# Windowed and pooled attention with a gated token mixer: query blocks of 122 with halo keys, band mask on GpSimd, transposed token mix, three-stage batch order

## The chip, the cores and the metric

The kernel runs on one core of a Trainium2 chip. The metric is the device time of one execution in microseconds (us). A core has TensorE (PE, matmuls, with a row of its own for weight loads, PEld), VectorE (DVE), ScalarE (ACT), GpSimd (POOL) and SyncE (SP), each with an instruction queue of its own that it works off in order. Matmuls write PSUM, the other engines read it and write SBUF.

## The reference

Eight batches of 576 tokens, 8 heads of 64. Attention has two parts that are added: one on tokens averaged in fours (144 positions, result repeated four times), one in which a token sees only tokens less than 4 away. The result, heads side by side, is `x` of a gated token mixer.

```python
q_d, k_d, v_d = (t.reshape(B, H, 144, 4, D).mean(axis=3) for t in (q, k, v))
out_up = np.repeat(sm_attn(q_d, k_d, v_d), 4, axis=2)      # softmax attention, scale 1/8
mask = np.abs(pos[:, None] - pos[None, :]) < 4
out_local = softmax(where(mask, q @ k.T / 8, -1e9)) @ v
x = (out_up + out_local), heads side by side: (8, 576, 512)
theta = x @ w_theta
y = w_tok_r @ (x * cos(theta)) + w_tok_i @ (x * sin(theta))   # over tokens, 576 x 576
u = x + y
out = u + maximum(u @ w_ch, 0)
```

## The kernel before, in words

All loads go through POOL's queue and turn float32 into bfloat16 on the way. First come the weights, then for each batch `q_tm`, `k_tm` and `v_tm`, 5 DMAs each (line 151), in pieces of 128 tokens on the partitions. `work` tiles have two buffers, so the load of batch b + 2 waits until batch b has used its tile.

`attention(b)` for one batch:

- Lines 165 and 170: for each pair of heads of q and k five transposes into `pstr` and, with the same data as weights, five matmuls against the pooling matrix `pool4` into `psd`. DVE copies both to SBUF (`sbT`, line 178, and `sbTd`, line 179).
- Line 191: pooled v, `psvd`. Lines 215 and 223: scores of the pooled attention `psSd` and their exps `pdT` on ACT, in key groups of 64 and 80 positions. Line 244: `psnd`, for each head two matmuls of 65 columns (64 of v and a column of ones for the sum), one with 64 and one with 80 rows of keys.
- Lines 276 to 295: for each of 5 key chunks of 128 (the last 64) the scores of up to 134 queries, `psS`, transposed: keys on partitions. Line 284 adds the band mask (0 or -1e9) by a matmul of the identity with `maskv`, four a chunk. ACT takes the exps into `pmain`.
- Line 314: `psup` repeats the pooled result fourfold by a matmul. Lines 338 and 340: `psloc`, the local result of a chunk of queries, four heads to a PSUM tile. A query near a chunk's start also needs the last keys of the chunk before: for chunks 1 to 4 every matmul with 128 (or 67) columns of weights is followed by one with 6, which adds into the first 6 rows. A matmul of zeros (`zrow`) closes the group.
- Lines 347 to 355: DVE divides by the sum and adds `psup`, giving `x`.

`moe(b)`: `x` is transposed (`xTps`, 369), theta is `psth` (386), cos and sin on ACT (394, 395), `zr` and `zi` on DVE, the token mix `psu` (412) is 5 output chunks of 10 matmuls of 512 columns, `u` on DVE (419), transposes `uTps` (428), `psr` (443), relu and sum on DVE (450), the write of `osb` on SP's queue (454).

The order is made by generators: each `yield` ends a step, and the loop at the end takes one step of `attention(b)`, one of `moe(b - 1)` and, at the start of a batch, up to 3 of `attention(b + 1)` in turn. The tile framework puts in the waits and may move instructions a little within an engine. PSUM has 8 banks: 6 tiles `w1` and 2 tiles `tr`.

## Time and profile before

| | us |
|---|---|
| median of 3 runs | 581.99 (580.44 to 582.56) |
| span of the profiled execution | 579.8 |
| PE busy | 529.4 (91%) |
| DVE, ACT, POOL busy | 256.9, 138.1, 115.6 |

PE stands for 82% of the chain of work that ended last. The sums for PE count time in which at least one matmul was in the pipeline, at whatever clock was granted; a granted clock of 1.00 is 2.4 GHz, 0.50 is 1.2 GHz.

### The profile page before, as it was taken

What the parts mean: (1) busy time and instruction counts of PE and PEld (TensorE: products, weight loads), DVE (VectorE), ACT (ScalarE), POOL (GpSimd) and SP (SyncE); (2) the same over time, 40 slices, a digit from 0 to 9 for tenths busy, and PEclk for the clock granted to TensorE, in tenths of its full rate; (3) what the DMA queues carried; (4) which work ended last, traced back from release to release, by engine and by line L of the source; (5) the groups of instructions that cost most, each with busy time, mean ns of one, the idle gap of its engine ahead of it and who ended that gap; (6) DMA issues with size and microseconds to landing.
All of it is one profiled execution on the core that took longest, in us unless ns stands there. A gap on an engine that the chain in (4) does not pass through costs nothing.

```text
span 579.8 us, 8334 instructions
## 1 busy us (share of the span) xinstructions
PE 529.4 (91%) x3386; PEld 291.3 (50%) x3386; DVE 256.9 (44%) x776; ACT 138.1 (24%) x384; POOL 115.6 (20%) x156
## 2 busy tenths in 40 slices
...
GB/s 81 173 144 143 22 55 2 81 15 69 42 36 46 75 42 9 82 36 48 41 42 42 72 17 35 1 3 80 42 1 0 37 47 0 1 9 74 2 6 75
DMA packets 120054, 26.50 MB, mean 46 GB/s; under 512 B 113232, under 2 KB 115408, under 8 KB 120016
## 3 DMA queue, kind: packets, MB, share of 16 engines
...
q14 instruction: 12, 0.10, 0.1%
...
## 4 chain that ended last, share of the span: by engine, by line
PE 82%; DVE 7%; DMA 6%; ACT 2%; POOL 1%; issue 1%; DVEq 0%; POOLq 0%
PE psu L412 22%; PE psloc L338 13%; PE psth L386 9%; PE psnd L244 7%; PE pstr L165 4%; PE psr L443 4%; DMA out_dram<-osb 4%; PE psup L314 3%; PE psd L170 3%; PE psS L284 3%; PE xTps L369 3%; PE psS L276 2%; PE psSd L215 2%; DVE sbT L178 2%; PE psvd L191 2%; PE psloc L340 2%
## 5 line engine op out<-in xcount | busy, mean ns | idle before, releaser
L338 PE MATMUL psloc<-v_tm,pmain 128*128 128x65 bf16 (+2 forms) x576 | 87.0, 218 | 4.4 <-DVE osb L450 4.4
L295 ACT ACTIVATE pmain<-psS 128x402 bf16<-128x402 f32 (+5 forms) x160 | 46.4, 375 | 171.8 <-PE psS L284 171.6
L419 DVE TENSOR_TENSOR u<-psu,x 128x512 bf16<-128x512 f32 (+2 forms) x40 | 27.6, 691 | 116.8 <-PE psu L412 116.8
L151 POOL DMA_DIRECT2D v_tm<-in_v_dram x40 | 33.9, 899 | 222.5 <-PE psloc L340 222.5
L338 PEld LDWEIGHTS <-pmain 128*128 128x128 bf16 (+2 forms) x576 | 54.9, 100 | 41.4 <-issue 12.5
L412 PE MATMUL psu<-zr,wrT 128*128 128x512 bf16 (+8 forms) x200 | 70.9, 502 | 0.0
L412 PE MATMUL psu<-zi,wiT 128*128 128x512 bf16 (+8 forms) x200 | 68.7, 489 | 0.0
L394 ACT ACTIVATE cos<-psth,pihc 128x512 bf16<-128x512 f32 (+2 forms) x40 | 28.0, 699 | 154.8 <-PE psth L386 154.8
L386 PE MATMUL psth<-wth,xT 128*128 128x512 bf16 (+2 forms) x160 | 56.8, 508 | 3.3 <-DVE xT L376 3.3
L223 ACT ACTIVATE pdT<-psSd 80x144 bf16<-80x144 f32 (+1 forms) x128 | 27.8, 285 | 84.7 <-PE psSd L215 84.2
L151 POOL DMA_DIRECT2D q_tm<-in_q_dram x40 | 34.2, 936 | 65.5 <-PE psSd L215 65.3
L443 PE MATMUL psr<-wch,uT 128*128 128x512 bf16 (+2 forms) x160 | 45.7, 388 | 1.0 <-DVE uT L435 0.3
L412 PEld LDWEIGHTS <-wiT 128*128 128x128 bf16 (+8 forms) x200 | 28.3, 142 | 36.2 <-issue 25.3
L450 DVE SCALAR_TENSOR_TENSOR osb<-psr,u 128x512 f32<-128x512 f32 (+2 forms) x40 | 27.1, 691 | 35.7 <-DMA out_dram<-osb 19.2
L244 PE MATMUL psnd<-vdext,pdT 64*72 64x65 bf16 (+1 forms) x256 | 42.5, 230 | 0.0
L178 DVE COPY sbT<-pstr 128x576 bf16<-128x576 bf16 x64 | 28.5, 453 | 25.6 <-PE pstr L165 20.6
L412 PEld LDWEIGHTS <-wrT 128*128 128x128 bf16 (+8 forms) x200 | 24.6, 137 | 25.3 <-issue 16.8
L347 DVE RECIPROCAL rl<-psloc 128x4 f32<-128x4 f32 (+2 forms) x80 | 14.3, 179 | 51.7 <-PE psloc L340 50.9
L244 PEld LDWEIGHTS <-pdT 64*72 64x72 bf16 (+1 forms) x256 | 29.1, 113 | 14.9 <-issue 3.7
L151 POOL DMA_DIRECT2D k_tm<-in_k_dram x40 | 34.4, 942 | 8.4 <-PE psd L170 8.4
L386 PEld LDWEIGHTS <-xT 128*128 128x128 bf16 (+2 forms) x160 | 20.8, 145 | 26.6 <-issue 12.1
L349 DVE TENSOR_TENSOR asm<-psloc,rl 128x256 bf16<-128x256 f32 (+2 forms) x80 | 30.5, 411 | 0.7
...
## 6 DMA issues: line engine op xcount, KB each, us to landing
...
```

The source lines that it names most:

```text
L151: nc.gpsimd.dma_start(out=dst[0:rows, c, :, 0:D], in_=src[b, :, 128 * c:128 * c + rows, :].rearrange("h p d -> p h d"),)
L178: nc.vector.tensor_copy(out=sb, in_=ps[:, 0:S])
L223: nc.scalar.activation(out=pd[0:kcnt, SD * (2 * hh + par):SD * (2 * hh + par) + SD], in_=psSds[hh][par][0:kcnt, :], func=AF.Exp, scale=SCL,)
L244: nc.tensor.matmul(out=psn[0:QD, 65 * hj:65 * hj + 65], lhsT=PdT[kk][0:kcnt, colbase:colbase + QD], rhs=vd_ext[kk].rearrange("p (h e) -> p ...
L295: nc.scalar.activation(out=outap[0:kw], in_=psSv[0:kw, :, :], func=AF.Exp, scale=SCL,)
L338: nc.tensor.matmul(out=o, lhsT=lt, rhs=rh, start=(imm == 0), stop=False)
L349: nc.vector.tensor_tensor(out=tmp[0:cnt, :], in0=plv[0:cnt, :, 0:D], in1=rl[0:cnt, 4 * beta:4 * beta + 4].unsqueeze(2).to_broadcast([cnt, ...
L386: nc.tensor.matmul(out=psth[0:cnt, :], lhsT=xT[dc][:, c, 0:cnt], rhs=wth[dc], start=(dc == 0), stop=(dc == 3),)
L394: nc.scalar.activation(out=ct[0:cnt], in_=psth[0:cnt], func=AF.Sin, bias=pihc[0:cnt], scale=1.0)
L412: nc.tensor.matmul(out=psu[0:cnt, :], lhsT=wt[0:TOK_CNT[g], TOK_START[c]:TOK_START[c] + cnt], rhs=zt[0:TOK_CNT[g], :], start=(j == 0), sto ...
L419: nc.vector.tensor_tensor(out=ut[0:cnt], in0=psu[0:cnt], in1=x_tiles[b][c][0:cnt], op=ALU.add)
L443: nc.tensor.matmul(out=psr[0:cnt, :], lhsT=uT[dc][:, c, 0:cnt], rhs=wch[dc], start=(dc == 0), stop=(dc == 3),)
```

## The change

- **Blocks of queries with their own keys.** The 576 queries are cut into blocks of 122 (`QS`, `QC`). Each block has its own window of up to 128 keys, from 3 before its first query to 3 after its last (`KS`, `KW`), so a block needs no keys of another. `psloc` has 8 matmuls a block, all of the same shape, and no closing matmul. v is loaded in these windows (`v_w`).
- **Band mask on POOL.** The mask matmuls are gone. ACT takes the exps of a block's 8 heads in one instruction, and two `affine_select` on POOL then write zeros on either side of the band.
- **Transposes and pooling in one matmul.** q and k are loaded 96 tokens to a piece; the matmul's moving operand `ip` is the identity and the pooling matrix side by side, 120 columns. ACT copies the transposed part, DVE the pooled one.
- **Pooled attention** in two equal key groups of 72; exps of three head pairs at once; pooled v by six masks `PM`.
- **Token mix transposed.** `psu` comes out with model columns on partitions and tokens along the free dimension, 288 at a time: the weights are `z`, the moving operand is the transposed token matrix `WT`. So `u` needs no transpose before `psr`; for the output it is transposed back (`psx`), relu goes to ACT, and DVE adds the two.
- **Order.** The batches run in three stages, `attention(b + 1)`, `modulate(b)` and `mix(b - 1)`, whose steps are taken in the order of the string `PERIOD`. The loads of a batch are issued when the attention of the batch before begins; those of batch 0 stand first in the program, ahead of the constants and the weights.
- **PSUM**: two tiles of two banks (`w2`: `pstr`, `psSd`, `psS`, `psnd`, `psloc`) and four of one (`w1`: all others).

```diff
 DM = 512
 SD = S // 4
 QD = 72
-NEG = -1.0e9
 PIH = math.pi / 2.0
 SCL = 1.0 / 8.0
 
-TOK_START = [0, 125, 253, 381, 509]
-TOK_CNT = [125, 128, 128, 128, 67]
+
+QS = [0, 122, 244, 366, 488]
+QC = [122, 122, 122, 122, 88]
+KS = [0, 119, 241, 363, 485]
+KW = [128, 128, 128, 128, 91]
+QN = [128, 128, 128, 128, 88]
 NCH = 5
-KW = [128, 128, 128, 128, 64]
-NCOL = [TOK_CNT[c] + (6 if c < 4 else 0) for c in range(NCH)]
-CW = 134
-KD_START = [0, 64]
-KD_CNT = [64, 80]
+TR = 96
+NTR = S // TR
+TP = TR // 4
+TW = TR + TP
+
+OS = [0, 128, 256, 384, 512]
+OC = [128, 128, 128, 128, 64]
 
...
-    psw = ctx.enter_context(tc.tile_pool(name="psw", bufs=6, space=bass.MemoryType.PSUM))
-    pst = ctx.enter_context(tc.tile_pool(name="pst", bufs=2, space=bass.MemoryType.PSUM))
+    ps2 = ctx.enter_context(tc.tile_pool(name="ps2", bufs=2, space=bass.MemoryType.PSUM))
+    ps1 = ctx.enter_context(tc.tile_pool(name="ps1", bufs=4, space=bass.MemoryType.PSUM))
+
...
+    def load(b):
+        q_tm = work.tile([TR, NTR, H, D], BF16, tag="q_tm", name=f"q_tm{b}")
+        k_tm = work.tile([TR, NTR, H, D], BF16, tag="k_tm", name=f"k_tm{b}")
+        v_w = work.tile([P, NCH, H, 66], BF16, tag="v_w", name=f"v_w{b}")
+        for dst, src in ((q_tm, q), (k_tm, k)):
+            for c in range(NTR):
+                nc.gpsimd.dma_start(
+                    out=dst[:, c, :, :],
+                    in_=src[b, :, TR * c:TR * c + TR, :].rearrange("h p d -> p h d"),
+                )
+        for c in range(NCH):
+            nc.gpsimd.dma_start(
+                out=v_w[0:KW[c], c, :, 0:D],
+                in_=v[b, :, KS[c]:KS[c] + KW[c], :].rearrange("h p d -> p h d"),
+            )
+        nc.vector.memset(v_w[:, :, :, 64:65], 1.0)
+        return q_tm, k_tm, v_w
+
+    inputs = {0: load(0)}
...
+    ip = const.tile([TR, TW], BF16, name="ip")
+    nc.vector.tensor_copy(out=ip[:, 0:TR], in_=ident[0:TR, 0:TR])
+    nc.gpsimd.memset(ip[:, TR:TW], 0.25)
+    nc.gpsimd.affine_select(out=ip[:, TR:TW], in_=ip[:, TR:TW], compare_op=ALU.is_ge, fill=0.0,
+                            base=0, pattern=[[-4, TP]], channel_multiplier=1)
+    nc.gpsimd.affine_select(out=ip[:, TR:TW], in_=ip[:, TR:TW], compare_op=ALU.is_ge, fill=0.0,
+                            base=3, pattern=[[4, TP]], channel_multiplier=-1)
...
+        if b + 1 < B:
+            inputs[b + 1] = load(b + 1)
...
+        for n, (tm, To, Tdo) in enumerate(((q_tm, qT, qdT), (k_tm, kT, kdT))):
+            for hh in range(4):
+                ps = w2(f"pstr{n}{hh}_{b}")
+                for c in range(NTR):
+                    nc.tensor.matmul(
+                        out=ps[:, c // 3, (c % 3) * TW:(c % 3) * TW + TW],
+                        lhsT=tm[:, c, 2 * hh:2 * hh + 2, :],
+                        rhs=ip,
                         start=True, stop=True,
+                    )
+                pv = ps[:, :, 0:3 * TW].rearrange("p k (c w) -> p k c w", w=TW)
+                nc.scalar.copy(
+                    out=To[:, hh, :].rearrange("p (k c w) -> p k c w", k=2, c=3),
+                    in_=pv[:, :, :, 0:TR],
+                )
+                nc.vector.tensor_copy(
+                    out=Tdo[:, hh, :].rearrange("p (k c w) -> p k c w", k=2, c=3),
+                    in_=pv[:, :, :, TR:TW],
+                )
+                yield
...
+        for kk in range(2):
+            ps = w2(f"psSd{kk}_{b}")
+            for hh in range(3):
+                pooled_scores(lambda par: ps[0:QD, par, SD * hh:SD * hh + SD], kk, hh)
+            nc.scalar.activation(
+                out=pd[:, kk, 0:6, :].rearrange("p (j e) w -> p e j w", e=2),
+                in_=ps[0:QD, :, 0:3 * SD].rearrange("p e (j w) -> p e j w", w=SD),
+                func=AF.Exp, scale=SCL,
+            )
...
+        pms = []
+        for c in range(NCH):
+            kw, qn = KW[c], QN[c]
+            ps = w2(f"psS{c}_{b}")
+            for hh in range(4):
                 for par in range(2):
+                    nc.tensor.matmul(
+                        out=ps[0:kw, par, P * hh:P * hh + qn],
+                        lhsT=kT[64 * par:64 * par + 64, hh, KS[c]:KS[c] + kw],
+                        rhs=qT[64 * par:64 * par + 64, hh, QS[c]:QS[c] + qn],
                         start=True, stop=True,
+                    )
+            pm = work.tile([P, 8, P], BF16, tag="pm", bufs=6, name=f"pm{c}_{b}")
+            nc.scalar.activation(
+                out=pm[0:kw, :, 0:qn],
+                in_=ps[0:kw].rearrange("p e (j w) -> p (e j) w", w=P)[:, :, 0:qn],
+                func=AF.Exp, scale=SCL,
+            )
+            off = KS[c] - QS[c] + 3
+            nc.gpsimd.affine_select(out=pm[0:kw, :, 0:qn], in_=pm[0:kw, :, 0:qn],
+                                    compare_op=ALU.is_ge, fill=0.0,
+                                    base=off, pattern=[[0, 8], [-1, qn]], channel_multiplier=1)
+            nc.gpsimd.affine_select(out=pm[0:kw, :, 0:qn], in_=pm[0:kw, :, 0:qn],
+                                    compare_op=ALU.is_ge, fill=0.0,
+                                    base=6 - off, pattern=[[0, 8], [1, qn]], channel_multiplier=-1)
+            pms.append(pm)
+            yield
...
+                    nc.tensor.matmul(
+                        out=pv[0:QD, h // 4, h % 4, :],
+                        lhsT=pd[:, kk, h, QD * g:QD * g + QD],
+                        rhs=vd[:, kk, h, 0:65],
+                        start=(h % 4 == 0 and kk == 0), stop=(h % 4 == 3 and kk == 1),
+                    )
...
+                nc.tensor.matmul(
+                    out=up[0:qn, :],
+                    lhsT=RT[g][:, QS[c]:QS[c] + qn],
+                    rhs=xd[:, g, :],
+                    start=(g == g0), stop=(g == g1),
+                )
+            ps = w2(f"psloc{c}_{b}")
+            pv = ps[:, :, 0:260].rearrange("p e (j w) -> p e j w", w=65)
+            for par in range(2):
+                for j in range(4):
+                    nc.tensor.matmul(
+                        out=pv[0:qn, par, j, :],
+                        lhsT=pms[c][0:kw, 4 * par + j, 0:qn],
+                        rhs=v_w[0:kw, c, 2 * j + par, 0:65],
+                        start=(j == 0), stop=(j == 3),
...
+            rl = work.tile([P, 2, 4], FP32, tag="rl", name=f"rl{c}_{b}")
+            nc.vector.reciprocal(out=rl[0:cnt], in_=pv[0:cnt, :, :, 64])
+            tmp = work.tile([P, DM], BF16, tag="tmp", name=f"tmp{c}_{b}")
+            nc.vector.tensor_tensor(
+                out=tmp[0:cnt].rearrange("p (j e d) -> p e j d", e=2, j=4),
+                in0=pv[0:cnt, :, :, 0:D],
+                in1=rl[0:cnt].unsqueeze(3).to_broadcast([cnt, 2, 4, D]),
+                op=ALU.mult,
+            )
+            x = xpool.tile([P, DM], BF16, tag="x", bufs=11, name=f"x{c}_{b}")
+            nc.vector.tensor_tensor(out=x[0:cnt], in0=tmp[0:cnt], in1=up[0:cnt], op=ALU.add)
+            xt.append(x)
...
+        uT = moep.tile([P, 4, S], BF16, tag="uT", name=f"uT{b}")
         for dc in range(4):
+            pss = [w1(f"psu{dc}{hf}_{b}") for hf in range(2)]
+            for c in range(NCH):
+                for ri in range(2):
+                    for hf in range(2):
+                        nc.tensor.matmul(
+                            out=pss[hf][:, 0:288],
+                            lhsT=z[0:QC[c], c, ri, P * dc:P * dc + P],
+                            rhs=WT[0:QC[c], ri, c, 288 * hf:288 * hf + 288],
+                            start=(c == 0 and ri == 0), stop=(c == NCH - 1 and ri == 1),
+                        )
+                if c == 2:
+                    yield
+            for hf in range(2):
+                nc.vector.tensor_tensor(
+                    out=uT[:, dc, 288 * hf:288 * hf + 288], in0=pss[hf][:, 0:288],
+                    in1=xT[:, dc, 288 * hf:288 * hf + 288], op=ALU.add,
+                )
+            yield
...
+            nc.scalar.activation(out=rel[0:cnt], in_=psr[0:cnt], func=AF.Relu)
+            osb = moep.tile([P, DM], FP32, tag="osb", bufs=3, name=f"osb{c}_{b}")
+            nc.vector.tensor_tensor(out=osb[0:cnt], in0=rel[0:cnt], in1=psx[0:cnt, 0:DM], op=ALU.add)
+            nc.sync.dma_start(out=out[b, OS[c]:OS[c] + cnt, :], in_=osb[0:cnt])
...
+    PERIOD = (
+        "m a a m x m a a m x m a a m x m a a m x m a m "
+        "a x a a a x a a x a a x a x a x a a x a a x a a x a x a"
+    ).split()
+
+    def run(a, m, x):
+        gens = {"a": a, "m": m, "x": x}
+        for s in PERIOD:
+            g = gens[s]
+            if g is not None:
+                next(g, 0)
+        for s in ("m", "x", "a"):
+            if gens[s] is not None:
+                drain(gens[s])
+
+    a0 = attention(0)
+    wt = build_WT()
+    for _ in range(10):
+        next(a0, 0)
+        next(wt, 0)
+    drain(wt)
+    drain(a0)
+    for b in range(B + 1):
+        run(attention(b + 1) if b + 1 < B else None,
+            modulate(b) if b < B else None,
+            mix(b - 1) if b >= 1 else None)
```

What stands on PE where local attention is computed, before: the end of one `psloc` tile, the `psup` of the next and its first matmuls (`pmain`: exps of a key chunk, two of them by turns; `rt`: the repeating matrix).

```order
L338 MATMUL psloc_3_3178<-v_tm_1856,pmain_3_3016 128x65
L338 LDWEIGHTS pmain_3_2987
L338 MATMUL psloc_3_3178<-v_tm_1856,pmain_3_2987 6x65
L340 LDWEIGHTS zrow
L340 MATMUL psloc_3_3178<-zrow 128x1
L314 LDWEIGHTS rt_107
L314 MATMUL psup_3_3188<-xd_3_2852,rt_107 128x256
L338 LDWEIGHTS pmain_3_3016
L338 MATMUL psloc_3_3190<-v_tm_1856,pmain_3_3016 128x65
L338 LDWEIGHTS pmain_3_2987
L338 MATMUL psloc_3_3190<-v_tm_1856,pmain_3_2987 6x65
```

And in the changed kernel, at the end of one `psloc` tile: `psloc` of attention for batch 2, `psr` of the mix for batch 0.

```order
L310 MATMUL psloc_2_1423<-v_w_571,pm_2_1266 128x65
L395 LDWEIGHTS uT_1022
L395 MATMUL psr_0_1438<-wch,uT_1022 128x512
...
L401 MATMUL psx_0_1443<-ident,uT_1022 128x128
L310 LDWEIGHTS pm_2_1279
L310 MATMUL psloc_2_1456<-v_w_571,pm_2_1279 128x65
...
L300 LDWEIGHTS rt_145
L300 MATMUL psup_2_1453<-xd_1333,rt_145 128x512
L300 LDWEIGHTS rt_149
L300 MATMUL psup_2_1453<-xd_1333,rt_149 128x512
```

The 6-column matmuls and the zero matmul between the others are gone, and whole groups of the mix of an earlier batch stand between the groups of attention.

On POOL, in the middle of the program, before:

```order
L151 DMA v_tm_1856<-in_v_dram 128x8x64 x4
L151 DMA v_tm_1856<-in_v_dram 64x8x64
L151 DMA q_tm_3380<-in_q_dram 128x8x64 x4
L151 DMA q_tm_3380<-in_q_dram 64x8x64
L151 DMA k_tm_3381<-in_k_dram 128x8x64 x4
L151 DMA k_tm_3381<-in_k_dram 64x8x64
```

And in the changed kernel (`pm_3` are the five blocks of batch 3, `v_w_1545` is v of batch 4, `q_tm_2116` and `k_tm_2117` are of batch 5):

```order
L82 DMA v_w_1545<-in_v_dram 128x8x64 x4
L82 DMA v_w_1545<-in_v_dram 91x8x64
L77 DMA q_tm_2116<-in_q_dram 96x8x64 x6
L77 DMA k_tm_2117<-in_k_dram 96x8x64 x6
L260 AFFINE_SELECT pm_3_1816<-pm_3_1816 128x1024
L260 AFFINE_SELECT pm_3_1839<-pm_3_1839 128x1024
L263 AFFINE_SELECT pm_3_1816<-pm_3_1816 128x1024
L263 AFFINE_SELECT pm_3_1839<-pm_3_1839 128x1024
L260 AFFINE_SELECT pm_3_1852<-pm_3_1852 128x1024
```

The selects stand in one queue with the loads of later batches, behind loads that wait for their buffers.

On DVE the tail of attention before, for chunks 2 and 3 of batch 2 (`x_2_243` and `x_3_244` are those chunks, `psloc` comes in halves of four heads):

```order
L347 RECIPROCAL rl_2_2377<-psloc_2_2394 128x4
L347 RECIPROCAL rl_2_2412<-psloc_2_2415 128x4
L349 TENSOR_TENSOR asm_2_2409<-psloc_2_2394,rl_2_2377 128x256
L349 TENSOR_TENSOR asm_2_2438<-psloc_2_2415,rl_2_2412 128x256
L355 TENSOR_TENSOR x_2_243<-asm_2_2409,psup_2_2391 128x256
L355 TENSOR_TENSOR x_3_244<-asm_2_2438,psup_2_2413 128x256
```

And in the changed kernel, for two blocks of batch 3 beside the output of batch 1:

```order
L317 RECIPROCAL rl_3_1988<-psloc_3_1979 122x8
L317 RECIPROCAL rl_3_2005<-psloc_3_1996 122x8
L319 TENSOR_TENSOR tmp_3_1990<-psloc_3_1979,rl_3_1988 122x2x4x64
L319 TENSOR_TENSOR tmp_3_2007<-psloc_3_1996,rl_3_2005 122x2x4x64
L326 TENSOR_TENSOR x_3_1992<-tmp_3_1990,psup_3_1977 122x512
L326 TENSOR_TENSOR x_3_2009<-tmp_3_2007,psup_3_1994 122x512
L407 TENSOR_TENSOR osb_1_2023<-rel_1_2021,psx_1_2016 128x512
L317 RECIPROCAL rl_3_2038<-psloc_3_2029 122x8
L317 RECIPROCAL rl_3_2055<-psloc_3_2046 122x8
L319 TENSOR_TENSOR tmp_3_2040<-psloc_3_2029,rl_3_2038 122x2x4x64
```

Each instruction now covers all 8 heads, blocks go in pairs, and an output sum of an earlier batch stands between the pairs.

## Rows read from the trace of the kernel before

**Rows 1.** The page: span, busy times, chain that ended last.

```profile
span 579.8 us, 8334 instructions
...
PE 529.4 (91%) x3386; PEld 291.3 (50%) x3386; DVE 256.9 (44%) x776; ACT 138.1 (24%) x384; POOL 115.6 (20%) x156
...
PE 82%; DVE 7%; DMA 6%; ACT 2%; POOL 1%; issue 1%; DVEq 0%; POOLq 0%
```

**Rows 2.** Windows: stretch, length, busy us of each engine (count), clock, DMA.

```profile
199.40:264.00 64.60, 62.61 (x419) 34.92 (x418) 31.07 (x96) 17.21 (x48) 12.60 (x15) 0.82 0.49 47
264.00:332.70 68.70, 66.74 (x419) 36.17 (x418) 31.07 (x95) 17.34 (x48) 12.59 (x15) 0.75 0.46 44
...
205.00:211.50 6.50, 6.50 (x41) 3.80 (x39) 3.14 (x11) 0.00 (x0) 0.00 (x0) 0.50 0.03 12
```

**Rows 3.** Timeline of PE, pieces: start, length, engine, line, what, count.

```profile
192.12 1.03 PE L443 MATMUL psr<-wch,uT 128*128 128x512 bf16 x4
193.08 0.41 PE L276 MATMUL psS<-sbT,sbT 64*128 64x134 bf16 x8
193.42 0.63 PE L284 MATMUL psS<-maskv,ident 128*128 128x402 bf16 x4
...
197.20 0.36 PE L338 MATMUL psloc<-v_tm,pmain 128*125 128x65 bf16 x4 [0.61 <-DVE osb L450]
...
200.58 1.10 PE L338 MATMUL psloc<-v_tm,pmain 128*128 128x65 bf16 x8
...
206.41 1.36 PE L338 MATMUL psloc<-v_tm,pmain 128*128 128x65 bf16 x8
...
228.92 2.34 PE L412 MATMUL psu<-zi,wiT 125*125 125x512 bf16 x5
...
242.80 2.46 PE L244 MATMUL psnd<-vdext,pdT 64*72 64x65 bf16 x16
...
250.93 1.25 PE L412 MATMUL psu<-zi,wiT 125*67 125x512 bf16 x5
...
252.91 0.57 PE L428 MATMUL uTps<-ident,u 128*128 128x128 bf16 x8
```

**Rows 4.** ACT: groups by shape (count, busy, mean ns, idle before), then timeline.

```profile
L295 ACT ACTIVATE pmain<-psS 128x402 bf16<-128x402 f32 x48 | 24.4, 509 | 35.5 <-PE psS L284 35.3
L295 ACT ACTIVATE pmain<-psS 128x134 bf16<-128x134 f32 x48 | 13.9, 290 | 0.3 <-PE psS L284 0.3
...
219.93 0.73 ACT L394 ACTIVATE cos<-psth,pihc 128x512 bf16<-128x512 f32 x1
220.50 0.64 ACT L395 ACTIVATE sin<-psth 128x512 bf16<-128x512 f32 x1
220.97 0.71 ACT L394 ACTIVATE cos<-psth,pihc 67x512 bf16<-67x512 f32 x1
...
222.19 1.28 ACT L223 ACT_TABLE_LOAD   x1
```

**Rows 5.** DVE: a group by shape, then two neighbours in the timeline.

```profile
L419 DVE TENSOR_TENSOR u<-psu,x 128x512 bf16<-128x512 f32 x24 | 16.6, 691 | 65.2 <-PE psu L412 65.2
...
261.07 1.35 DVE L450 SCALAR_TENSOR_TENSOR osb<-psr,u 128x512 f32<-128x512 f32 x2 [2.60 <-DMA out_dram<-osb]
```

**Rows 6.** Timeline of POOL: selects of constants, the load of one tensor.

```profile
2.29 0.29 POOL L71 TENSOR_SCALAR_AFFINE_SELECT maskv<-maskv 128x140 bf16<-128x140 bf16 x1
2.70 0.66 POOL L95 TENSOR_SCALAR_AFFINE_SELECT rt<-rt 72x576 bf16<-72x576 bf16 x1
...
21.31 4.23 POOL L151 DMA_DIRECT2D k_tm<-in_k_dram  x5
```

**Rows 7.** First and last batch's first theta matmuls, last output sum (timeline, chain).

```profile
79.26 0.69 PE L386 MATMUL psth<-wth,xT 128*125 128x512 bf16 x1 [0.26 <-DVE xT L376]
...
542.37 0.85 PE psth L386 x2
...
570.42 0.69 DVE L450 SCALAR_TENSOR_TENSOR osb<-psr,u 67x512 f32<-67x512 f32 x1 [1.59 <-DMA out_dram<-osb]
```

More of the change, by code (lines that the diff above doesn't have):

```diff
@@ new lines, in attention @@
+                nc.scalar.copy(
[7 more added lines that the diff above has]
+                yield
+        vd = work.tile([QD, 2, H, 66], BF16, tag="vd", name=f"vd{b}")
+        nc.vector.memset(vd[:, :, :, 64:65], 1.0)
```

496 lines of the change are left out of this document (136 added, 360 removed).

## The prediction

> **What bounds the kernel now.** I read the page first: TensorE (PE) is busy 529.4 of 579.8 us and 82% of the chain that ended last is its own work, so PE is the bound [rows 1]. The windows then give one steady batch: of 64.6 us PE is busy 62.6, VectorE (DVE) 31.1, ScalarE (ACT) 17.2, GpSimd (POOL) 12.6 [rows 2]. Nothing but PE matters here, and DVE, ACT and POOL have room. The first theta matmul starts at 79.26 and the last batch's at 542.37, so seven batches take 463.1 us, 66.2 each; 79.3 lie ahead and 37.4 behind [rows 7].
>
> The timeline shows that a busy PE is not a PE at its peak. psnd does 16 matmuls of 65 columns in 2.46 us, 0.15 us each. psloc does 8 in 1.10, 0.13 each, and 1.36 (0.17 each) in a stretch at the lower clock level of 1.2 GHz. But the four psloc matmuls of chunk 0 go at 0.05 each [rows 3]. They have the same 65 columns and about the same weights. What differs is the shape: in chunks 1 to 4 every second matmul is 6 columns wide in its weights, in psnd every second one has 64 or 80 rows, in chunk 0 all are alike. So I read the 0.13 to 0.17 as the price of changing shape from matmul to matmul, not of 65 columns. That weight loads are hidden is shown by uTps: 8 matmuls of 128 columns in 0.57 us, 0.05 each [rows 3]. PE's clock falls as well: PE is busy throughout 205 to 211.5 us, in psloc, at a granted 0.50 [rows 2], and the psu matmuls after it then need 2.34 us for five instead of 1.25 [rows 3].
>
> **What the change does to PE.** Per batch it removes 32 six-column matmuls and 10 one-column ones of psloc, the 20 mask matmuls (0.63 us for four, [rows 3]), and 40 pooling matmuls, which now ride in the transposes (48 of 120 columns for 80). psloc is left with 40 and psnd with 32, each set of nearly one shape. Priced by chunk 0's row, psloc falls from 10 groups of 1.1 to 1.4 us to 40 x 0.05 = 2 us, psnd from 32 x 0.15 = 4.8 to 1.6. The token mix turns from 50 x 512 columns into 80 x 288, 10% fewer. At 2.4 GHz, one column per cycle (512 columns 0.213 us, as psr and psu show), a batch of the new kernel is: psu 80 x 0.12 = 9.8; psth and psr 20 x 0.215 = 4.3 each; psvd and psup 6 x 0.215 = 1.3 each; transposes 48 + 20 + 20 at 0.055 = 4.8; psS 20 pairs at 0.06 (8 in 0.41, [rows 3]) = 1.2; psSd 0.5; psloc and psnd 3.6. That is 31.1 us. Four psr matmuls take 0.96 us up to the next row's start, 0.1 more than 4 x 0.215 [rows 3]: I add 0.1 for each of some 60 changes of group, so PE needs 37 us. All of it at 1.2 GHz would be some 66.
>
> So PE ceases to be far above the others, and waits begin to count. **ACT** gains the q and k copies, the v copy and the relu. Its exps of 402 and 134 elements take 509 and 290 ns, 0.82 ns per element over 180 [rows 4]; but neighbours overlap, one cos-sin pair follows the other after 1.04 us [rows 4], so 512 elements cost about 0.52, 576 0.55, 1024 0.92. Per batch: 8 copies 4.4, pairs 5.2, two table loads 2.6, v 1.0, pooled exps 2.1, band exps 4.4, relu 2.6: 22 us. **DVE**: 512 elements from PSUM take 691 ns alone and follow each other after 0.65 [rows 5]; some 23 us. **POOL**: one tensor's load of 576 rows takes 4.2 us [rows 6], three 12.7. The band mask is new: ten selects. Selects of 140 and 576 elements take 0.29 and 0.66 us [rows 6], a line of 0.18 + 0.84 ns per element, so 1.04 us for 1024 and 9.8 a batch. No row has a select with a repeated inner pattern; below, the line's slope alone gives 8.6, above, I take double, 19.6; the line is nearest.
>
> **A full run** (three batches in flight) goes by the hand-written order:
> - *Four quarters* (a transpose group, two q/k groups, a theta group, half a psu step): PE 13.8 us with changes of group; ACT needs 8.5. Twice a transpose waits for a PSUM buffer that the psu sum's add still holds, then the theta matmuls wait for DVE's copy behind z: 0.65 each, 2.6 in all. Less 1.2 that the tail already covers: 15.2. Then psvd, psSd and the last theta: 2.9.
> - *Exps*: from the last theta ACT does a pair, a table load, the pooled exps and four band exps before psnd gets its buffer: 1.04 + 1.28 + 2.1 + 3.7 = 8.2. PE's 7.8 of work (half of psu, psS) hides beside it.
> - *Tail*: psnd, two psr groups and the first psloc, 5.0; then DVE sets the pace: 16 operations of 0.6 between the first psloc and the next theta, with three short ones and a copy, 10.2. PE has 7.5 to do there. Together 15.2.
>
> Sum 41.5 us at full clock. POOL's 22.5 hide: the q and k loads end before the first band exp, the ten selects start 5.3 after the last theta and end at 15.1, and the last psloc comes after 17. With the cover gone, each us of selects beyond 17 is a us per run.
>
> The clock I do not put at full: mean 0.92, above the 0.82 of the batch in [rows 2], since what drew it down there (psloc with its changing shapes) is what goes. With 16% of the time at the lower level, a run is 1 / (0.84/41.5 + 0.16/66) = 44 us.
>
> **Ahead and behind.** The loads of batch 0 now precede everything on POOL: 0.7 + 12.7. Constants follow, about 10 us (six pooling masks of four selects, two of 576), six weight DMAs 6, then batch 1's load, 12.7, and only then batch 0's selects, queued behind it: 42 + 9.8, and 2.5 for the last psloc and its sums: 54.5 us instead of 79.3. The next run has no mix; its band exps begin 17.2 later, selects end at 81.5, the run at 84. Then six full runs, 264. Then theta and mix without attention: PE 20.4 + 4.6 of changes and waits = 25. Last the mix of batch 7: 16.2, relu and add 1.2, write about 2, and the 8.7 from the last osb's end to the span's end [rows 7]: 28. Span 84 + 264 + 25 + 28 = 401; the median of the runs, 581.99, lies 2.2 above the profiled 579.8, so 403.
>
> **The rivals.**
> 1. *The clock does not recover.* For it: PE now has small waits in every quarter and in the tail, and the next batch of before has a mean of 0.75 [rows 2]. Against: dense psu and psr now stand among the small matmuls. At the old mean of 0.82 (36% at the lower level) a run is 47.9: 427 us. At the lower level throughout, 66: some 570. The Trainium skill (TensorE: Matmul & The Clock Gate, "A second HAM failure mode") says that cycling through PSUM banks with short idles between groups makes the clock swing; by that rule the first of these two results comes out. In the trace so far the swings stand around psloc, theta and the first psu matmuls.
> 2. *Small matmuls stay dear.* If 65 columns cost 0.13 to 0.15 whatever the shapes, psnd and psloc are 6 us longer a run, of which the tail's slack takes half: 425.
> 3. *POOL is slower than its line.* At 2.07 a select, the first two phases grow by 9.8 each and every full run by 3.6: 444. The Trainium skill (GPSIMD Engine Reference, "Elementwise — side-by-side cycle accounting") gives 1.8 cycles per element for a tight software loop at 1.2 GHz and advises against elementwise work there; an estimate from it is 1.5 us a select, and by that the time would be about 423. The 576-element row shows 0.66 us, less than that figure gives, so the row stands.
> 4. *Slower than before*, the same mechanism further out: POOL as the bound of every run. A time of 582 needs runs of 74 us, (74 - 12.7)/10 = 6.1 us a select, six times the line. It decides only there; nothing in the rows points to it.
> 5. *Better*: fewer waits between the queues than I count, runs of 39 or less: below 372.
>
> **Chances.** Forecast 0.55, rival 1 0.20, rival 2 0.10, rival 3 0.08, rival 5 0.05, rival 4 or no change 0.02. The range from 372 to 455 takes in rivals 1 (first form) to 3 and leaves out about 2 in 10. A measurement of this kernel can tell 0.5% from no change. Faster by more than that 0.97, within 0.015, slower 0.015.
>
> **What will show it.** Right: psloc groups of 8 in about 0.5 us, psnd 16 in about 1; PE busy near 85% of a run of 44; a granted clock near 0.9; select rows of 1.0 us; PE idle ended by DVE in the tail and by ACT before psnd; first theta near 55. Wrong: full runs over 48 us with a clock under 0.85 (rival 1), spacing over 0.1 in psloc (rival 2), selects over 1.5 us or PE idle before psloc ended by POOL (rival 3), or an engine other than DVE holding the tail.

## The result, and the profile after

The changed kernel takes 364.8 us (median of four runs, 362.1 to 365.5) for 582.3 before: a ratio of 0.626, 95% interval 0.622 to 0.629. The forecast was 403 with a range from 372 to 455, so the change is faster as forecast, but the time lies below the range: the gain was put 38 us too small. The profiled execution took 365.0, its span is 363.3. From its page (span; busy time, share and instructions of each engine; the granted clock in 40 slices; the chain that ended last), beside [rows 1]:

```profile
span 363.3 us, 6945 instructions
...
PE 293.9 (81%) x2820; PEld 199.3 (55%) x2834; DVE 180.7 (50%) x428; ACT 191.3 (53%) x280; POOL 202.5 (56%) x267
...
PEclk9999955975699999999999999999999999989999
...
PE 45%; DVE 17%; ACT 15%; POOL 14%; issue 4%; DMA 4%; DVEq 0%; POOLq 0%
```

PE is no longer the whole chain, and its clock is low for long only in slices 6 to 11 of 40 (45 to 100 us). Windows with the columns of [rows 2]: up to the first theta, the run without a mix, the first full run, a steady run, theta and mix without attention, the last mix:

```profile
0.00:61.91 61.91, 27.92 (x248) 20.48 (x249) 15.72 (x44) 14.12 (x19) 53.34 (x98) 0.88 1.19 99
61.91:92.48 30.57, 23.03 (x237) 16.05 (x235) 16.59 (x41) 20.61 (x31) 30.46 (x37) 0.72 1.35 87
92.48:132.35 39.87, 36.35 (x349) 23.95 (x348) 22.27 (x55) 24.95 (x37) 27.13 (x32) 0.93 0.94 81
...
169.68:206.98 37.30, 33.77 (x346) 22.66 (x349) 21.70 (x53) 24.00 (x36) 23.54 (x28) 1.00 0.85 82
318.71:342.30 23.59, 21.74 (x148) 14.51 (x150) 9.80 (x20) 7.85 (x14) 0.00 (x0) 0.93 0.07 20
342.30:363.30 21.00, 16.61 (x127) 11.53 (x128) 8.12 (x16) 3.97 (x7) 0.00 (x0) 1.00 0.28 98
```

Against the forecast: the first full run begins at 92.5 for 84 (+8.5); six full runs take 226.2 for 264 (-37.8); the two last stretches 44.6 for 53 (-8.4); what lies around the span 1.7 for 2.2. That is the whole of the 38 us. The steady run is the large one: 37.3 for 44. The late start hides part of that miss. Its pieces in the timeline of PE (columns as in [rows 3]):

```profile
169.68 1.07 PE L352 MATMUL psth<-wth,xT 128*122 128x512 bf16 x4 [1.02 <-DVE xT L348]
...
176.71 1.07 PE L352 MATMUL psth<-wth,xT 128*122 128x512 bf16 x4 [0.86 <-DVE xT L348]
...
185.06 0.25 PE L213 MATMUL psSd<-qdT,kdT 64*72 64x144 bf16 x2
...
193.75 0.71 PE L276 MATMUL psnd<-vd,pd 72*72 72x65 bf16 x16
...
195.73 1.03 PE L395 MATMUL psr<-wch,uT 128*128 128x512 bf16 x4
196.60 0.39 PE L401 MATMUL psx<-ident,uT 128*128 128x128 bf16 x4
196.82 0.38 PE L300 MATMUL psup<-xd,rt 72*128 72x512 bf16 x1
197.04 0.40 PE L310 MATMUL psloc<-v_w,pm 128*128 128x65 bf16 x8
197.29 0.38 PE L300 MATMUL psup<-xd,rt 72*128 72x512 bf16 x1
```

From the first theta to the end of the last (185.06) it is 15.4 us, forecast 18.1; from there to psnd 8.7, forecast 8.2; from psnd to the next first theta (206.98) 13.2, forecast 15.2. In the last five rows each start follows the one ahead without a gap: the next group starts 0.87 us after four psr (4 x 0.2175), 0.22 after four psx, 0.22 after psup, 0.25 after eight psloc. The 0.1 that I had added for each change of group is not there. psloc (8 in 0.40) and psnd (16 in 0.71) were 1.1 to 1.4 and 2.46 before [rows 3].

In the tail (psnd to the next theta) VectorE does not stop from 197.43 until the next theta. Its timeline:

```profile
197.43 0.69 DVE L407 TENSOR_TENSOR osb<-rel,psx 128x512 f32<-128x512 f32 x1
...
199.48 1.27 DVE L326 TENSOR_TENSOR x<-tmp,psup 122x512 bf16<-122x512 bf16 x2
...
203.90 0.68 DVE L407 TENSOR_TENSOR osb<-rel,psx 128x512 f32<-128x512 f32 x1
...
206.53 0.40 DVE L348 COPY xT<-xTps 128x488 bf16<-128x488 bf16 x1
```

The prologue is where the time is longer than forecast. Its timeline, POOL first, then PE:

```profile
34.20 1.53 POOL L77 DMA_DIRECT2D q_tm<-in_q_dram  x2 [2.55 <-DMA wtm<-in_moe_w_tok_r_dram]
...
41.77 3.81 POOL L77 DMA_DIRECT2D k_tm<-in_k_dram  x5 [2.85 <-DMA wch<-in_moe_w_ch_dram]
...
49.93 2.19 POOL L260 TENSOR_SCALAR_AFFINE_SELECT pm<-pm 128x1024 bf16<-128x1024 bf16 x2
...
33.95 3.94 PE L154 MATMUL wps<-ident,wtm 128*122 128x128 bf16 x25 [8.01 <-DMA wtm<-in_moe_w_tok_r_dram]
```

Two queues wait for the weights to land: POOL within batch 1's load, 7.4 us in four waits (two of them shown), ahead of batch 0's selects; and PE, 8.0 us, ahead of batch 0's band scores.

### The profile page after: what moved, and what is told of

Read it like the earlier page. It is cut to its first block, busy times and chain, and to the rows that moved or that the text cites. A ratio compares the mean times of both kernels' runs of the same rounds, so it can differ in the third digit from the quotient of the medians.

```text
span 363.3 us, 6945 instructions
## 1 busy us (share of the span) xinstructions
PE 293.9 (81%) x2820; PEld 199.3 (55%) x2834; DVE 180.7 (50%) x428; ACT 191.3 (53%) x280; POOL 202.5 (56%) x267
## 4 chain that ended last, share of the span: by engine, by line
PE 45%; DVE 17%; ACT 15%; POOL 14%; issue 4%; DMA 4%; DVEq 0%; POOLq 0%
PE psu L377 16%; PE psth L352 10%; PE psr L395 5%; DVE tmp L319 4%; DVE osb L407 4%; DMA wch<-in_moe_w_ch_dram 4%; ACT pd L224 3%; DVE x L326 3%; ACT cs L359 3%; PE psS L247 3%; POOL pm L260 3%; POOL k_tm L77 3%; ACT L224 2%; PE pstr L177 2%; PE psvd L199 2%
## 5 line engine op out<-in xcount | busy, mean ns | idle before, releaser
L377 PE MATMUL psu<-WT,z 122*128 122x288 bf16 (+1 forms) x640 | 94.2, 292 | 0.0
L260 POOL TENSOR_SCALAR_AFFINE_SELECT pm<-pm 128x1024 bf16<-128x1024 bf16 (+1 forms) x40 | 40.7, 1038 | 71.4 <-ACT pm L254 71.3
L377 PEld LDWEIGHTS <-z 122*128 122x128 bf16 (+1 forms) x640 | 60.0, 99 | 23.8 <-issue 0.5
L352 PE MATMUL psth<-wth,xT 128*122 128x512 bf16 (+1 forms) x160 | 44.6, 402 | 14.2 <-DVE xT L348 14.2
L386 DVE TENSOR_TENSOR uT<-psu,xT 128x288 bf16<-128x288 f32 x64 | 27.3, 454 | 53.2 <-PE psu L377 53.2
L77 POOL DMA_DIRECT2D q_tm<-in_q_dram x48 | 37.0, 789 | 15.4 <-PE pstr L177 10.0
L361 DVE TENSOR_TENSOR z<-cs,x 122x1024 bf16<-122x1024 bf16 (+1 forms) x40 | 27.4, 686 | 34.3 <-ACT cs L360 34.3
L77 POOL DMA_DIRECT2D k_tm<-in_k_dram x48 | 36.8, 779 | 13.0 <-PE pstr L177 10.1
L395 PE MATMUL psr<-wch,uT 128*128 128x512 bf16 (+1 forms) x146 | 40.5, 380 | 2.3 <-DVE x L326 1.6
L254 ACT ACTIVATE pm<-psS 128x1024 bf16<-128x1024 f32 (+1 forms) x40 | 35.3, 976 | 12.5 <-PE psS L247 12.0
L263 POOL TENSOR_SCALAR_AFFINE_SELECT pm<-pm 128x1024 bf16<-128x1024 bf16 (+1 forms) x40 | 40.7, 1038 | 0.4
L82 POOL DMA_DIRECT2D v_w<-in_v_dram x40 | 35.4, 913 | 9.7 <-PE psloc L310 7.3
L359 ACT ACTIVATE cs<-psth,pihc 122x512 bf16<-122x512 f32 (+1 forms) x40 | 27.6, 691 | 23.7 <-PE psth L352 23.3
```

The costliest lines, as they stand in the source:

```text
L77: nc.gpsimd.dma_start(out=dst[:, c, :, :], in_=src[b, :, TR * c:TR * c + TR, :].rearrange("h p d -> p h d"),)
L82: nc.gpsimd.dma_start(out=v_w[0:KW[c], c, :, 0:D], in_=v[b, :, KS[c]:KS[c] + KW[c], :].rearrange("h p d -> p h d"),)
L254: nc.scalar.activation(out=pm[0:kw, :, 0:qn], in_=ps[0:kw].rearrange("p e (j w) -> p (e j) w", w=P)[:, :, 0:qn], func=AF.Exp, scale=SCL,)
L260: nc.gpsimd.affine_select(out=pm[0:kw, :, 0:qn], in_=pm[0:kw, :, 0:qn], compare_op=ALU.is_ge, fill=0.0, base=off, pattern=[[0, 8], [-1, qn ...
L263: nc.gpsimd.affine_select(out=pm[0:kw, :, 0:qn], in_=pm[0:kw, :, 0:qn], compare_op=ALU.is_ge, fill=0.0, base=6 - off, pattern=[[0, 8], [1, ...
L352: nc.tensor.matmul(out=th[0:cnt, :], lhsT=xT[:, dc, QS[c]:QS[c] + cnt], rhs=wth[:, dc, :], start=(dc == 0), stop=(dc == 3),)
```

## The experiments

Times are medians of four runs; "run" is a steady full run, from first theta to first theta, with its granted clock.

| kernel | us | run, us | clock |
|---|---|---|---|
| before | 582 | 64.4 to 69.0 | 0.75 to 0.82 |
| before, like shapes together | 497.8 | 53.5 to 59.0 | 0.82 to 0.90 |
| changed | 364.8 | 37.3 | 1.00 |
| six columns, 64 keys, alternating | 492.4 | 54.2 to 57.7 | 0.71 to 0.78 |
| the same, like shapes together | 379.7 | 39.5 | 1.00 |
| 72 columns, 66 keys, alternating | 362.5 | 37.5 | 1.00 |
| no hand-written order | 418.6 | 45.7 to 46.7 | 0.79 to 0.80 |
| selects twice | 424.3 | 44.4 to 45.4 | 0.92 to 0.96 |
| one select of two left out | 363.1 | 37.3 | 1.00 |
| mask on PE | 372.9 | 39.1 | 1.00 |
| tmp twice | 387.8 | 39.7 to 41.7 | 0.87 to 1.00 |
| weights' transposes late | 365.3 | 37.3 | 1.00 |
| loads late | 364.5 | 37.3 | 1.00 |
| both, and constants first | 349.5 | 37.3 | 1.00 |
| the same, transposes spread | 349.0 | 37.3 | 1.00 |
| the same, z partly on GpSimd | 346.3 | 36.6 | 1.00 |

### Shapes and the clock

**The kernel before, like shapes together.**

```diff
-for hj in range(4):
-    for kk in range(2):        # psnd
+for kk in range(2):
+    for hj in range(4):
+if c >= 1:                     # psloc
+    mms = mms[0::2] + mms[1::2]
```

> The kernel before with the same matmuls in another order: in psnd the four with 64 rows first and then the four with 80, in psloc the four wide ones first and then the four of six columns. Theory (a change of shape from matmul to matmul costs 0.1 us): a psloc group of chunks 1 to 4 falls from 1.1 to 1.4 us to about 0.5, psnd from 0.15 us a matmul to about 0.06, together 9 us a batch: some 510 us; if the alternation also drew the clock down, the mean granted clock rises from 0.80 to 0.9 or more and the time falls further, to some 470. Rival (65 columns are dear in any order): spacings and time as before, 582 us within 1%. Rival on the clock: the time falls by the spacings alone and the clock stays near 0.80.

497.8 us, ratio 0.856 (0.851 to 0.862). Two of its steady runs (windows), and psnd and one psloc group (timeline of PE):

```profile
125.81:179.34 53.53, 51.12 (x417) 28.81 (x417) 30.77 (x96) 17.20 (x48) 12.61 (x16) 0.90 0.59 56
236.58:295.55 58.97, 54.92 (x417) 30.92 (x417) 30.80 (x96) 17.20 (x48) 12.26 (x16) 0.82 0.53 51
...
210.91 1.09 PE L244 MATMUL psnd<-vdext,pdT 64*72 64x65 bf16 x16
...
228.85 0.51 PE L340 MATMUL psloc<-v_tm,pmain 128*128 128x65 bf16 x8
229.29 0.17 PE L342 MATMUL psloc<-zrow 1*128 1x1 bf16 x1
```

Eight psloc matmuls now take 0.44 us up to the next row, 16 of psnd 1.09 in all: the price lay in the order. The same matmuls in another order are worth 82 us of the old kernel. The mean clock rose from 0.80 only to 0.87, short of the 0.9 expected, so the alternation is not all that drew it down there; what else does was not tried.

**The old shapes put back into the changed kernel**, three ways with the same number of matmuls (psnd and psloc):

```diff
-lhsT=pd[:, kk, h, ...]
+lhsT=pd[0:QD - 8 * kk, kk, h, ...]
 ...
+if j < 3:
+    nc.tensor.matmul(out=pv[0:6, par, j, :],
+        lhsT=pms[c][0:kw, 4 * par + j, 0:6],
+        rhs=v_w[0:kw, c, 2 * j + par, 0:65], start=False, stop=False)
```

> The changed kernel with the shapes of before put back: behind three of four psloc matmuls comes one of six columns (it doubles the first six queries' sums and their denominators alike), and every second psnd matmul takes 64 of the 72 keys (8 pooled keys are left out). Theory (a change of shape costs 0.1 us): 7 psloc matmuls need 0.98 us for 0.20, psnd 16 in 2.4 for 0.71: +11 us a steady run of PE time, run 47 for 37.3, time some 445 us; if alternation lowers the clock, the steady runs' granted clock falls from 1.00 to under 0.9 and the time is nearer 470. Rival (order is free): +0.03 us for each added matmul, 0.9 us a run, time 365 to 375. Rival on the clock: longer, but still 1.00.

Grouped: the same, with the three added ones together ahead of the fourth wide one, and `kk` as psnd's outer loop.

> The same matmuls as in the kernel with alternating shapes, 8 pooled keys left out in the same way, but like shapes stand together: three six-column matmuls in a row within each psloc group, psnd's eight of 72 rows and then its eight of 64. Theory: two changes of shape in a psloc group for six, one in psnd for fifteen: +0.3 us a psloc group, 3 us a run of PE time, partly covered by waits in the tail: 370 to 390 us, steady clock 1.00. Rival (it is the added matmuls, not their order): the same time as the alternating one.

Large: the alternating order with `0:72` for `0:6` and `6 * kk` for `8 * kk`.

> As the kernel with alternating shapes, matmul for matmul and in the same order, but the added psloc matmuls have 72 columns of weights instead of 6 (they double the first 72 queries' sums and denominators alike), and every second psnd matmul takes 66 of the 72 keys instead of 64 (6 pooled keys are left out). Theory A (it is a step across 64 rows, or down to a few columns, that costs 0.1 us; unlike shapes on one side of it follow each other at 0.03): steady runs 38 to 40, granted clock 1.00, time 368 to 385 us, like the grouped kernel's 380. Theory B (any change of shape costs): 55 us a run at a clock near 0.73, time 492 us, like the alternating kernel's.

Alternating 492.4, grouped 379.7, large 362.5 us. The alternating one: a steady run (window), its stretch from first theta to psnd, and the next 25.8 us; then psnd and the start of psloc (timeline of PE):

```profile
166.30:222.00 55.70, 53.74 (x379) 32.31 (x379) 22.46 (x53) 23.60 (x36) 23.57 (x27) 0.73 0.58 55
166.30:190.35 24.05, 22.86 (x215) 15.49 (x216) 9.10 (x24) 18.67 (x28) 11.90 (x15) 1.00 1.03 71
190.35:216.10 25.75, 25.75 (x135) 13.62 (x133) 10.75 (x23) 2.97 (x5) 7.26 (x8) 0.53 0.09 32
...
190.35 2.69 PE L276 MATMUL psnd<-vd,pd 72*72 72x65 bf16 x16
...
200.33 0.26 PE L310 MATMUL psloc<-v_w,pm 128*128 128x65 bf16 x1
200.52 0.22 PE L317 MATMUL psloc<-v_w,pm 128*6 128x65 bf16 x1
```

The grouped one:

```profile
176.76:216.27 39.51, 36.67 (x379) 24.54 (x379) 22.08 (x53) 23.99 (x36) 23.57 (x28) 1.00 0.81 77
...
200.80 0.83 PE L276 MATMUL psnd<-vd,pd 72*72 72x65 bf16 x16
...
204.52 0.25 PE L317 MATMUL psloc<-v_w,pm 128*128 128x65 bf16 x3
204.71 0.25 PE L311 MATMUL psloc<-v_w,pm 128*6 128x65 bf16 x3
```

The one with large alternating shapes:

```profile
170.50:207.97 37.47, 34.77 (x378) 23.66 (x378) 21.83 (x53) 23.99 (x36) 23.61 (x28) 1.00 0.85 81
...
194.62 0.71 PE L276 MATMUL psnd<-vd,pd 72*72 72x65 bf16 x16
...
197.91 0.19 PE L310 MATMUL psloc<-v_w,pm 128*128 128x65 bf16 x1
197.94 0.20 PE L317 MATMUL psloc<-v_w,pm 128*72 128x65 bf16 x1
```

Theory A stands: alternating 66 with 72 rows, or 72 with 128 columns, costs nothing (0.03 us from start to start). Alternating 64 with 72 rows makes 16 psnd matmuls 2.69 us long for 0.71; alternating 6 with 128 columns, the starts lie 0.14 to 0.19 apart. These psloc rows stand at 1.2 GHz, where like ones are 0.06 apart (eight in 0.46 us, 84.12 to 84.58 in the changed kernel's run without a mix). The grouped rows show the price at 2.4 GHz: three wide matmuls take 0.19 us up to the first of six columns, for 3 x 0.03, so a change costs 0.1. Up to psnd the alternating run equals the changed kernel's (24.05 and 24.07). Then the granted clock falls to 1.2 GHz, 1.5 us into psnd and with PE busy 25.75 of 25.75 us: alternation costs twice, once by itself and once by the clock. The 470 expected had counted on a clock under 0.9; it fell to 0.73. So the fall needs no time in which the profile counts PE as idle; but a PE with one matmul in its pipeline counts as busy, and what in the alternation lowers the clock was not tried.

### What hides what in a run

**No hand-written order**: theta, mix and attention are drained one after the other.

```diff
-for s in PERIOD:
-    g = gens[s]
-    if g is not None:
-        next(g, 0)
 for s in ("m", "x", "a"):
```

> The changed kernel without the hand-written order: in each run theta, mix and attention of the three batches are written out one after the other. Theory (the interleaving hides ACT's and DVE's chains, which I priced at waits of some 10 us a run where nothing else is there to do): PE idle ended by ACT and DVE grows from 3.5 to about 13 us a run, run 47, time 440 to 450 us. Rival (the engines overlap anyway, since each takes its own instructions as they become ready): under 3% more, below 376 us.

418.6 us, for 440 to 450 expected. One run in four windows: theta, mix, scores and exps, the sums:

```profile
187.10:196.40 9.30, 8.40 (x63) 5.59 (x61) 5.11 (x14) 8.02 (x13) 6.97 (x9) 0.83 1.55 98
196.40:213.90 17.50, 17.45 (x139) 12.19 (x138) 8.52 (x18) 5.89 (x12) 0.06 (x1) 1.00 0.43 76
213.90:222.50 8.60, 4.04 (x57) 2.90 (x57) 0.31 (x1) 8.35 (x11) 7.30 (x9) 0.71 1.16 88
222.50:232.95 10.45, 9.26 (x94) 6.75 (x94) 8.66 (x21) 1.23 (x2) 9.22 (x11) 0.50 0.03 3
```

The run is 46, near the 47 expected, but for another reason: PE's idle time is 6.7 us a run, not 13. In the third window PE waits for ACT's exps, busy 4.04 of 8.60; there the clock falls, and the sums after it run at 1.2 GHz. The order saves 8.6 us in this run: 3.2 of it is idle time of PE (6.7 for 3.5), 5.4 is the same matmuls taking longer (PE busy 39.2 for 33.8) at a clock of 0.80.

**Selects doubled, and one of two left out.**

```diff
+for _ in range(2):
     nc.gpsimd.affine_select(out=pm[0:kw, :, 0:qn], ..., base=off, ...)
     nc.gpsimd.affine_select(out=pm[0:kw, :, 0:qn], ..., base=6 - off, ...)
```

> The changed kernel with each pair of band selects issued twice. Theory of the prediction (selects begin at a fixed time after the last theta and have 1.9 us of cover in a steady run): first theta 9.8 us later, the first run without mix 9.8 longer, each of six full runs and the first of the two last +8, idle of PE before psloc ended by POOL: about 440 us, run 45. Rival 1 (POOL wholly hidden in steady runs): only the two first phases grow, 385 us, run 37.3. Rival 2 (POOL sets the pace of a run by its sum, now 34 of 37.3 us): runs of 37 to 38 and 390 us.

```diff
-nc.gpsimd.affine_select(out=pm[0:kw, :, 0:qn], ..., base=6 - off, ...)
```

> The changed kernel with one of the two band selects of each chunk left out, so that only one edge of the band is masked. Theory (selects have 2 us of cover in a steady run, since doubling them cost 7.4 of 9.4 us): steady runs stay at 37.3, the first run without mix ends 4.9 earlier: 360 us. Rival (POOL is on the path of every run): 4.9 us less in each of eight runs, 326 us.

424.3 and 363.1 us. Doubled, a batch's selects last from 223.81 to 244.0, 20.2 us for 10.1, and the steady run grows by 7.4 of these 10.1: 2.7 us of cover where the prediction had 1.9. The total is 15 below the expected one, since the two first phases together grow by 12.4 for 19.6, and I had counted a run that has no attention. With one left out the steady run is 37.30 as before: GpSimd is off its path. Ahead of it the first full run begins 1.4 us earlier, not the 4.9 expected.

**The mask back on TensorE**, with `maskv` 0 in the band and -1e9 outside, and no selects.

```diff
+for par in range(2):
+    nc.tensor.matmul(
+        out=ps[0:kw, par, :].rearrange("p (j w) -> p j w", w=P)[:, :, 0:qn],
+        lhsT=ident[:, 0:kw],
+        rhs=maskv[:, 3 - off:3 - off + qn].unsqueeze(1).to_broadcast([P, 4, qn]),
+        start=False, stop=True)
 ...
```

> The changed kernel with one part undone: the band mask goes back to TensorE, two 512-column matmuls of a mask row per chunk added to the scores, and no selects on GpSimd. Theory (selects are covered in steady runs, TensorE is not): PE +2.1 to 3 us a run, of which some three quarters shows, as with the grouped kernel's added matmuls: run 39.0 to 39.6, +13 to 18 us over eight phases; ahead of the steady runs no selects wait behind batch 1's load: first full run 8 to 12 us earlier. Together 366 to 375 us. Rival (the mask on GpSimd is what makes the run short): run above 42, time above 385 us. Rival (mask matmuls beside the scores draw the clock down): clock of the steady runs below 0.95.

372.9 us. Run +1.8: the selects' move to GpSimd is worth 1.8 us a run, and mask matmuls alone leave the clock at 1.00. The time is within the 366 to 375 expected, but ahead of the steady runs the first full run begins at 91.2, only 1.3 earlier, not 8 to 12. PE's wait for the weights, 6.84 us there, holds batch 0's band scores whatever GpSimd does.

**tmp twice.**

```diff
+for _ in range(2):
     nc.vector.tensor_tensor(out=tmp[0:cnt]..., op=ALU.mult)
```

> The changed kernel with the multiply that makes tmp issued twice for each chunk: 5 x 0.65 us more of VectorE between the first psloc and the next theta. Theory of the prediction (VectorE sets the pace of that stretch, 10.2 us): +3.2 us a run, run 40.5, time 391 us, PE idle before the next theta ended by DVE. Rival (PE is the bound of the whole run and VectorE has slack there): under 1 us a run, 365 to 372 us.

387.8 us. Runs at full clock take 39.7, +2.4 for 3.2 added: VectorE sets the tail's pace. Later runs at a clock of 0.87 to 0.96 take 40.1 to 41.7.

### The prologue

**One cause each.** First the token weights' transposes into the first run:

```diff
-for _ in range(10):
-    next(a0, 0)
-    next(wt, 0)
-drain(wt)
 drain(a0)
-    mix(b - 1) if b >= 1 else None)
+    mix(b - 1) if b >= 1 else wt)
```

> The changed kernel with the token weights' transposes written into the first run, not ahead of it; GpSimd's queue as it was. Theory (two queues each waited some 8 us for the weights' DMAs in the prologue, TensorE ahead of batch 0's band scores and GpSimd within batch 1's load, one behind the other's back, so that mending one alone brings little): batch 0's selects still start near 50 behind batch 1's load, first theta 58 to 61, first full run 90 to 94, time 361 to 367 us. Rival (TensorE's wait is the whole prologue miss): first theta near 53, time 356 us.

Then the loads of batches 1 and 2 behind the selects of the batch ahead:

```diff
-if b + 1 < B:
+if 2 <= b and b + 1 < B:
     inputs[b + 1] = load(b + 1)
 ...
 pms.append(pm)
+if b < 2 and c == NCH - 1:
+    inputs[b + 1] = load(b + 1)
```

> The changed kernel with only the loads of batches 1 and 2 moved behind the selects of the batch ahead of each; the token weights' transposes stay ahead of batch 0's band scores on TensorE. Theory (as above): batch 0's exps still wait for these transposes until 46, its selects end near 55, first theta 50 to 54, but batch 1's load then starts at 55 and ends at 68, and the first full run begins at 90 to 96: time 362 to 368 us. Rival (GpSimd's wait is the whole miss): first full run near 80, time 350 us.

365.3 and 364.5 us: each alone brings nothing. First the one with the transposes late, then the one with the loads late (timelines of PE):

```profile
52.32 0.62 PE L310 MATMUL psloc<-v_w,pm 128*128 128x65 bf16 x8 [13.94 <-POOL pm L263]
```

```profile
34.46 3.94 PE L154 MATMUL wps<-ident,wtm 128*122 128x128 bf16 x25 [8.48 <-DMA wtm<-in_moe_w_tok_r_dram]
```

With one wait gone the other queue is late at the same place. (With the loads late the first theta came at 59.9, not 50 to 54, since batch 1's transposes, which waited for their load, stand ahead of it on PE.)

**Both, and `ident` and `ip` ahead of batch 0's load.**

```diff
-inputs = {0: load(0)}
 ident = const.tile([P, P], BF16, name="ident")
 ...
 ip = const.tile([TR, TW], BF16, name="ip")
 ...
+inputs = {0: load(0)}
```

> The changed kernel with GpSimd's queue in another order ahead of the steady runs: the identity and the transposes' constant ahead of batch 0's load, the loads of batches 1 and 2 behind the band selects of the batch ahead of each, and the token weights' transposes in the first run instead of ahead of it. Theory (the first theta came 7.4 us later than forecast because batch 1's load, ahead of batch 0's selects on GpSimd, waited for the weights' DMAs to land): first theta at 42 to 45 us for 61.9, the first full run begins near 72 for 92.7, steady runs 37.3, time 345 us. Rival (the DMAs themselves bound the prologue, whatever stands in GpSimd's queue): first theta after 50, time above 355 us.

349.5 us, ratio 0.602 (0.599 to 0.606). First theta at 37.8, first full run at 76.9 for 92.5, steady runs untouched. The third move was not tried without the other two. An estimate of its share: batch 0's selects begin at 28.83 here, right behind the last weight's issue; with the transposes late and `ident` behind the load, the first band exp runs from 30.12 to about 31.1, so the move brings some 2.3 of the 15 us. Then the transposes spread, one `wt` step behind each theta step of the first run:

```diff
+def both(a, c):
+    for _ in a:
+        next(c, 0)
+        yield
-modulate(b) if b < B else None,
-mix(b - 1) if b >= 1 else wt)
+modulate(b) if b >= 1 and b < B else both(modulate(0), wt) if b == 0 else None,
+mix(b - 1) if b >= 1 else None)
```

> The kernel with GpSimd's queue reordered, and in it the token weights' transposes of the first run spread between the theta groups instead of 25 of them standing ahead of the last pooled scores. Theory (those 2.7 us of TensorE hold up the exps and with them the first select of batch 1): first full run begins at 74 to 75 for 76.9, time 347 us. Rival (the loads of batch 1 set it): no change, 349.5.

349.0: no gain. The pooled exps still begin at 59.9 us, behind ACT's v copies, last cos-sin pair and table load.

**z of chunks 1 and 3 on GpSimd**, from batch 2, in the same kernel:

```diff
-nc.vector.tensor_tensor(
+(nc.gpsimd if c in (1, 3) and b >= 2 else nc.vector).tensor_tensor(
     out=z[0:cnt, c, :, :], ...
```

> The same, and in batches 2 to 7 the z multiply of chunks 1 and 3 goes from VectorE to GpSimd. Theory (the two waits of a theta group for VectorE's copy of xT, 1.0 and 0.9 us a steady run, stand behind z on VectorE): 1 to 1.5 us less in each of five or six runs, steady run 36, time 339 to 342 us. Rival (GpSimd's multiply is long and delays the loads that stand behind it, or slows VectorE): steady run 37.3 or more, time 347 or above.

346.3 us, ratio 0.597 (0.592 to 0.602), the fastest of all. A steady run (window) and z's group on GpSimd (count, busy, mean ns):

```profile
154.84:191.45 36.61, 33.55 (x349) 22.60 (x349) 20.59 (x51) 23.93 (x36) 27.79 (x31) 1.00 0.87 83
...
L363 POOL TENSOR_TENSOR z<-cs,x 122x1024 bf16<-122x1024 bf16 x12 | 25.6, 2129 | 42.6 <-ACT cs L362 25.8 <-PE pstr L177 12.0 <-DVE uT L388 4.7
```

The second of the two waits for xT fell from 0.86 to 0.26, the first stayed at 1.02, so the gain is 0.7 us a run, about half of that expected, and the time lies above the 339 to 342 expected.

## Why the prediction missed

- **What bounds before, and the price of shapes: right.** The reading that changing shapes and not 65 columns made psloc and psnd dear stands, and the orders show it: 82 us in the kernel before, 113 between the alternating and the grouped one (492.4 and 379.7). Not every change is dear, though: 66 with 72 rows is free. psloc at 2 us a batch and psnd at 1.6 were foreseen; five groups of 0.25 and two of 0.7 came. Rival 2 falls. What the merged transposes, the transposed token mix and the larger exps bring was not tried apart.
- **PE 37 us at full clock: the step that failed first.** 60 changes of group at 0.1 made 6 of the 37; PE is busy 33.8 in a steady run. The one row it came from, 0.96 for four psr [rows 3], had a change to psS's 64 rows behind it, a dear one. The same trace of before has four psr ahead of psup's 72 rows (timeline of PE), and there they take 0.87, with nothing added:

```profile
195.45 1.04 PE L443 MATMUL psr<-wch,uT 128*128 128x512 bf16 x4
196.32 0.27 PE L314 MATMUL psup<-xd,rt 72*125 72x256 bf16 x1
```

  Most changes in the new order cost nothing either. This is most of the 15.4 for 18.1 (PE is busy 14.4 there, for 16.7 forecast) and of the 3.5 from psnd to the end of the first psloc, for 5.0. With the tail's 0.5 less and the exps' 0.5 more, a run is 37.3 for the 41.5 of full clock, 4.2 us less. A smaller slip went the other way: psS was put at 0.06 a pair from a row that gives 0.34 us for four pairs up to the next start [rows 3], 0.085; it hides beside the exps.
- **Mean clock 0.92: the second.** I kept a sixth of each run at the lower level though what I held responsible was to go, and no row gave the sixth. The steady runs show 1.00: 2.5 us a run (44 for 41.5). Rival 1 did not come, but waits can lower the clock in this kernel: the run without the hand-written order shows 0.80, and falls where PE waits. Rival 1's rule in the Trainium skill (TensorE: Matmul & The Clock Gate, "A second HAM failure mode"), by which short idles between groups in changing PSUM banks make the clock swing, does not agree with the steady runs, which have idles of 0.2 to 1.0 us and 1.00; nor does it name the fall with PE busy throughout, which the alternating kernel shows.
- **Tail paced by VectorE: right**, 9.7 for 10.2 from the end of the first psloc (197.29) on; doubling tmp shows it. **Exps: right**, 8.7 for 8.2.
- **Selects of 1.04 us, hidden: right.** The timeline has 1.04 from start to start; the cover is 2.7 for 1.9. Rivals 3 and 4 fall. The Trainium skill's figure (GPSIMD Engine Reference, "Elementwise — side-by-side cycle accounting"; the estimate from it was 1.5) does not agree with the 1.04 us. Rival 3's price was too low by the prediction's own rule: 5.3 + 19.6 - 17 is 7.9 us a run, not 3.6, and the doubled selects cost 7.4; at that price it lay above the range that was to take it in.
- **Prologue 54.5: too short.** Every DMA issue was priced, none of the landings that later work waits for, and of the two queues that wait only GpSimd's was looked at: 61.9 came. This error of 8.5 us up to the first full run, the other way, made the whole miss look smaller: without it it is near 47.
- **The end: too long.** The last osb ends at 360.1, 3.2 us ahead of the span's end, for the 8.7 taken over from [rows 7]; that is 5.5 of the 8.4. There osb had waited for an earlier write; why the last write was longer was not tried.
- **The range.** Rival 5, fewer waits and runs of 39 or less, had 0.05. It was the same count of changes and waits seen from the other side; the margin laid on both should have stood in the range as a bound of its own.
